# A recurrent attention with a gated feed-forward layer: the first running maxima spread from stacked halves, queries of one chunk instead of two in padded windows, and a new order

## The chip, the core and the metric

The kernel runs on one core of a Trainium2 chip. The core's engines work side by side, each through its own queue in strict program order: TensorE (PE in the profile; its weight loads are PEld) does matrix products and transposes into accumulators (PSUM), VectorE (DVE) and ScalarE (ACT) do elementwise work on accumulators and SBUF, GpSimd (POOL) does elementwise work on SBUF alone, SyncE (SP) issues most transfers. They wait for one another by semaphores. The metric is the device time of one execution in microseconds, the median of the runs.

## The reference

Inputs are q, k, v and an output gate, each [4 batches, 8 heads, 768 steps, 40], input and forget gates [4, 8, 768], and three feed-forward matrices. What matters of it:

```python
for t in range(S):
    m_new  = np.maximum(f_gate[:, :, t] + m, i_gate[:, :, t])
    f_stab = np.exp(f_gate[:, :, t] + m - m_new)
    i_stab = np.exp(i_gate[:, :, t] - m_new)
    C = f_stab * C + i_stab * outer(v[t], k[t])      # 40 x 40 for each batch and head
    n = f_stab * n + i_stab * k[t]
    y[t] = sigmoid(o_gate[t]) * (C @ q[t]) / max(|n . q[t]|, 1)
    m = m_new
x   = y as [4 * 768 tokens, 320]
out = (sigmoid(x @ w_gate) * (x @ w_val)) @ w_out    # 320 -> 1536 -> 320
```

## The kernel before

The 768 steps are cut into six chunks of 128. A unit is one batch in one chunk, numbered n = 4 * chunk + batch, so units 0 to 3 are chunk 0 and 4 to 7 chunk 1. In a unit the recurrence becomes products: scores of keys and queries (tile s), multiplied by a decay matrix d = exp(at - running maximum) with a triangular mask, and that times the values (tile av); from chunk 1 on the incoming state (tile cst) times the queries is added (tile in, the incoming term, line 740 on). The result is divided and gated (den, av, x), transposed (xt) and split into a high and a low part (xh, xl) of a type that TensorE takes in one pass. The feed-forward layer follows in tiles of 256 or 512 tokens: 16 or so products into two accumulators (pg, line 902), tanh on ScalarE and the gate product on VectorE (sg, lines 915 and 918), again a high and a low part (gh, gl), and the products with w_out (po, line 940). The weights arrive as 64-bit numbers and are decoded by ScalarE and VectorE (dc, lines 507 to 520) and split (wh, wl, w, oh, ol, lines 545 to 567).

The heads of 40 columns stand in three groups of 3, 3 and 2, so that a group fills 120 or 80 of the 128 rows. For units below EU = 8 keys and queries are transposed on TensorE (line 605 for keys, 607 for queries). The queries of these units lie in a tile qpad with zeros around each head; a window of that tile, transposed, holds one head of a group and zeros for the others (function window), so that a group needs one transpose for keys and as many for queries as it has heads. Tile sop (names kq) holds both, and one score product does a whole group (lines 719 and 1049). The incoming term of these units takes one product per head (line 749). Later units get keys and queries turned by VectorE and by transfers through memory, and qk holds a whole group's queries at once; there the incoming term takes one product per group (line 746), because cst has zeros between the heads.

At the start the gates of chunk 0 are summed up and their running maximum m0 (32 rows: batch and head) is found by scans on VectorE (gates_first). The maximum of a head is then spread to all 128 rows by a product with a column of the identity, four heads to an accumulator (function spread in opening, line 1024, tiles mb), from which ScalarE makes the decay (line 1029). TensorE gets products on a zero tile between its first real ones (keep_warm, `iq`, line 1003, twelve pairs of records; warming, `im`, six products).

Nothing is scheduled while it runs. Every step is put in a list under a key (`put`), and the table ORDER names the keys in the order in which the instructions are issued. PARAM['eng'] says for a step which engine does it: `v` VectorE, `a` ScalarE, `p` GpSimd.

Of the kernel before, what the change touches and what calls it, by code (L numbers as in the profile page):

```python
# [1151 lines left out]
```

## Time and profile before

| | us |
|---|---|
| median of 3 runs | 522.73 (522.59 to 523.77) |
| the profiled execution | 523.94 |
| its span, first to last instruction | 522.2 |
| TensorE busy | 514.5 |
| VectorE busy | 315.2 |
| ScalarE busy | 208.3 |
| GpSimd busy | 159.9 |

The profiled execution took 1.74 us more than its span and 1.2 us more than the median. In the views a row of the timeline gives a start, a duration, the engine, the line of the kernel, the operation, output and inputs with shapes, and a count of records. TensorE's records of one product overlap, so that the spacing in the chain of waits, not the duration of a record, is what a product costs in a row of them. An ordinary 32-bit product leaves two records, a transpose one.

### The profile page before, as it was taken

To read this page: it belongs to the slowest core of one execution; us is meant where nothing else is said; L and a number is where in the kernel's file an instruction comes from. 1 tells how busy PE (TensorE), PEld (TensorE's weight loads), DVE (VectorE), ACT (ScalarE), POOL (GpSimd) and SP (SyncE) were. 2 spreads that over 40 slices of the span, in tenths; PEclk is the share of its full clock that TensorE was granted. 3 is DMA by queue.
4 is the path that set the end of the run, shared out by engine and by line. 5 is a ranking of instruction groups with operands and counts; after the bars stand their busy time and mean duration, and the time that the engine had idled before them with its cause. 6 is when DMAs were issued, how large, how long until landed. Compare 5 with 4: busy or idle time off the path is not lost.

```text
span 522.2 us, 12322 instructions
## 1 busy us (share of the span) xinstructions
PE 514.5 (99%) x4747; PEld 468.6 (90%) x4747; DVE 315.2 (60%) x746; ACT 208.3 (40%) x535; POOL 159.9 (31%) x220
## 2 busy tenths in 40 slices
PE   8999999999999999999999999999999999999997
PEld 7788988888999999998888888898888888999997
DVE  6999879886556657656647544555456444342222
ACT  4786576673441433342433341223423131222321
POOL 3433244146444122305234425233322121202110
PEclk9999999999999999999999999999999999999999
DMA  8977776586778598688958799686689741000000
GB/s 197 239 223 195 196 199 211 134 156 130 183 147 188 125 196 165 162 155 177 187 139 184 156 178 198 150 179 126 142 173 191 162 87 48 28 13 2 32 9 25
DMA packets 227578, 75.55 MB, mean 145 GB/s; under 512 B 207040, under 2 KB 215424, under 8 KB 227520
## 3 DMA queue, kind: packets, MB, share of 16 engines
q1 hardware_dynamic: 226432, 74.51, 64.1%
q8 instruction: 37, 0.61, 0.5%
q10 hardware_dynamic: 1088, 0.26, 0.3%
q14 instruction: 21, 0.17, 0.1%
HBM read 57.61 MB, written 17.14 MB: 143 GB/s over the span
## 4 chain that ended last, share of the span: by engine, by line
PE 94%; DVE 3%; DMA 1%; issue 1%; POOL 0%; ACT 0%; DVEq 0%; POOLq 0%
PE pg L902 52%; PE po L940 25%; PE av L702 3%; PE s L724 2%; PE cs L855 2%; PE in L746 2%; PE s L719 1%; PE xt L820 1%; PE in L749 1%; PE pt L607 1%; PE mb L1024 1%; DMA d<-mscr 1%; PE s L1049 1%; DMA gin<-in_f_gate_dram 1%; PE pt L605 0%
## 5 line engine op out<-in xcount | busy, mean ns | idle before, releaser
L915 ACT ACTIVATE sg<-pg 128x256 f32<-128x256 f32 (+1 forms) x103 | 48.4, 470 | 211.6 <-PE pg L902 196.4
L929 POOL TENSOR_TENSOR gl<-sg,gh 128x256 fp32r<-128x256 f32 (+1 forms) x54 | 54.3, 1005 | 199.5 <-ACT gh L923 94.5
L918 DVE SCALAR_TENSOR_TENSOR sg<-sg,pg 128x256 f32<-128x256 f32 (+1 forms) x103 | 53.9, 523 | 95.8 <-ACT sg L915 54.1
L902 PE MATMUL pg<-xh,wh 128*128 128x256 f32 (+1 forms) x412 | 109.5, 336 | 0.1
L902 PE MATMUL pg<-xh,wl 128*128 128x256 f32 (+1 forms) x412 | 107.7, 328 | 0.0
L902 PE MATMUL pg<-xl,wh 128*128 128x256 f32 (+1 forms) x412 | 105.7, 329 | 0.0
L940 PE MATMUL po<-oh,gh 128*128 128x320 f32 x288 | 88.5, 321 | 0.0
L940 PE MATMUL po<-oh,gl 128*128 128x320 f32 x288 | 86.8, 317 | 0.0
L940 PE MATMUL po<-ol,gh 128*128 128x320 f32 x288 | 86.1, 314 | 0.0
L902 PEld LDWEIGHTS pg<-xh,wl 128*128 128x128 f32 x412 | 70.0, 188 | 5.2
L902 PEld LDWEIGHTS pg<-xl,wh 128*128 128x128 f32 x412 | 68.9, 188 | 5.2
L902 PEld LDWEIGHTS pg<-xh,wh 128*128 128x128 f32 x412 | 69.1, 188 | 4.8 <-DVE sg L918 0.3
L902 PE MATMUL pg<-xl,w 128*128 128x256 f32 (+1 forms) x206 | 62.0, 331 | 0.0
L940 PEld LDWEIGHTS po<-oh,gh 128*128 128x128 f32 x288 | 53.2, 188 | 3.8
L940 PEld LDWEIGHTS po<-ol,gh 128*128 128x128 f32 x288 | 53.2, 188 | 3.5
L940 PEld LDWEIGHTS po<-oh,gl 128*128 128x128 f32 x288 | 53.1, 188 | 2.9
L902 PE MATMUL pg<-xh,w 128*128 128x256 f32 (+1 forms) x206 | 54.4, 330 | 0.0
L923 ACT ACTIVATE gh<-sg 128x256 fp32r<-128x256 f32 (+1 forms) x65 | 32.2, 495 | 45.0 <-DVE sg L918 28.1
L730 DVE TENSOR_TENSOR d<-s,d 128x384 f32<-128x384 f32 (+1 forms) x66 | 32.8, 506 | 26.3 <-PE s L724 22.9
L462 ACT ACTIVATE d<-d,at 128x128 f32<-128x128 f32 x136 | 42.4, 391 | 0.1
L929 DVE TENSOR_TENSOR gl<-sg,gh 128x256 fp32r<-128x256 f32 (+1 forms) x49 | 28.6, 584 | 17.8 <-ACT gh L923 9.3
L902 PEld LDWEIGHTS pg<-xl,w 128*128 128x128 f32 x206 | 36.9, 188 | 1.8
(162 smaller groups left out, 728.1 us busy)
## 6 DMA issues: line engine op xcount, KB each, us to landing
d<-mscr SPq DMA_DIRECT2D x22, 512.0 KB
k<-in_k_dram SPq DMA_DIRECT2D x24, 160.0 KB
v<-in_v_dram SPq DMA_DIRECT2D x24, 160.0 KB
o<-in_o_gate_dram SPq DMA_DIRECT2D x24, 160.0 KB
st_o<-in_moe_w_out_dram SPq DMA_DIRECT2D x12, 320.0 KB
scr0q<-qt SPq DMA_DIRECT2D x32, 120.0 KB
...
```

The costliest lines, as they stand in the source:

```text
L462: nc.scalar.activation(d[:, h, :], d[:, h, :], AF.Exp, bias=at[:, c, b * H + h : b * H + h + 1], scale=-1.0)
L702: nc.tensor.matmul(dst[xs], lhs[:, xs], rhs, start=True, stop=True)
L724: nc.tensor.matmul(ps[g][:, m, :], ks[: 3 * D, h0 + m, :], qs[: 3 * D, h0 + m, :], start=True, stop=True)
L730: nc.vector.tensor_tensor(x, ps[g][:, :nh, :], x, ALU.mult)
L746: nc.tensor.matmul(pi[:, h0 : h0 + nh, :], qk[u][:r, g, :], cst[:r, b, g, : nh * DA], start=True, stop=True)
L855: nc.tensor.matmul(ps[0][:r, g, : nh * DA], kt[u][:, h0 : h0 + nh, :].rearrange("p h d -> p (h d)"), vt[u][:, h0 : h0 + nh, :], start=True ...
L902: nc.tensor.matmul(pg[x], w[:, a, fs] if a < 2 else w[:, fs], y[c][:, a, n0:n1], start=first, stop=a == 2 and y is xl)
L915: nc.scalar.activation(sg[0], pg[0], AF.Tanh, scale=0.5)
L918: nc.vector.scalar_tensor_tensor(sg[0], sg[0], 1.0, pg[1], ALU.add, ALU.mult)
L923: nc.scalar.activation(gh[u][:, :nt], sg[0], AF.Copy)
L929: E('gl0' if c == 0 else 'gl', f'tl{n}').tensor_tensor(gl[u][:, :nt], sg[0], gh[u][:, :nt].bitcast(F32), ALU.subtract)
L940: nc.tensor.matmul(po[t], g[c, j, t0][:, (t - t0) * P : (t - t0 + 1) * P], o[:, j, :], start=j == 0 and first, stop=j == NF - 1 and last)
```

## The change

1. *First maxima.* The running maximum is stored twice in a tile mm of the single-pass type: rows 0 to 31 hold its rounded value, rows 32 to 63 the rest (steps `ih`). A selector pick2 has a one in row h and in row 32 + h (step `iy`), so that one product with it adds both parts and spreads a head's maximum.
2. *Queries.* PU = 4 is new: only units 0 to 3 use padded windows. For units 4 to 7 a group's queries are transposed once, copied to qk, and multiplied by the mask rmask (one value per row and head of the group) into sop (steps `aq`); scores work as before. Their incoming term takes one product per group, and line 749 goes.
3. *Masks.* The mask cmask for the state is replaced by rmask, broadcast.
4. *Warm products.* keep is 7 instead of 12, warm 1 instead of 6.
5. *Order.* ORDER is a new table, with nine more steps than before (fifteen new, six gone), and 267 entries of PARAM['eng'] differ.

```diff
     'eng': {
...
-        'cm1': 'a', 'cp00': 'a', 'cp02': 'a', 'qb2': 'v', 'ro': 'v', 'xd0': 'v', 'bk0': 'v', 'cx0': 'p', 'bk1': 'v',
+        'cm1': 'a', 'cp00': 'v', 'cp02': 'v', 'qb2': 'v', 'ro': 'v', 'xd0': 'v', 'bk0': 'v', 'cx0': 'p', 'bk1': 'v',
...
-            if x < PARAM['EU']:
+            if x < PARAM['PU']:
                 return qpad[x % 2]
-            s = x % 6
+            s = (x - PARAM['PU']) % 6
...
+    mm = const.tile([P, L], F32R, name="mm")
+    pick2 = const.tile([P, BH], F32R, name="pick2")
...
+        def halves():
+            nc.vector.tensor_copy(mm[:BH], m0[:BH])
+
+        def rest():
+            nc.vector.tensor_tensor(mm[BH : 2 * BH], m0[:BH], mm[:BH].bitcast(F32), ALU.subtract)
...
-        for m in range(nh):
-            nc.tensor.transpose(p[:r, 1 + m, :], window(u, g, m), ident)
+        nc.tensor.transpose(p[:r, 0, :], heads(kt), ident)
+        if padded(u):
+            for m in range(nh):
+                nc.tensor.transpose(p[:r, 1 + m, :], window(u, g, m), ident)
+        else:
+            nc.tensor.transpose(p[:r, 1, :], heads(qt), ident)
...
+            pairs = [(sop[u][:r, g, 0], p[:r, 0]), (qk[u][:r, g], p[:r, 1])]
+        for dst, part_ in pairs:
+            if eng == "v":
+                nc.vector.tensor_copy(dst, part_)
+            else:
+                nc.scalar.activation(dst, part_, AF.Copy)
+
+    def spread(u, g, key):
+        nh = GROUPS[g][1]
+        r = nh * D
+        E(f'qb{g}', key).tensor_tensor(sop[u][:r, g, 1 : 1 + nh, :], qk[u][:r, g, :].unsqueeze(1).broadcast_to([r, nh, L]),
+                                      rmask[:r, :nh].unsqueeze(2).broadcast_to([r, nh, L]), ALU.mult)
...
-                if u in qk:
-                    nc.tensor.matmul(pi[:, h0 : h0 + nh, :], qk[u][:r, g, :], cst[:r, b, g, : nh * DA], start=True, stop=True)
-                    continue
-                for m in range(nh):
-                    nc.tensor.matmul(pi[:, h0 + m, :], sop[u][:r, g, 1 + m, :], cst[:r, b, g, m * DA : (m + 1) * DA],
-                                     start=True, stop=True)
+                nc.tensor.matmul(pi[:, h0 : h0 + nh, :], qk[u][:r, g, :], cst[:r, b, g, : nh * DA], start=True, stop=True)
...
-                cm = cmask.rearrange("p j e -> p (j e)")[:r, :w].unsqueeze(1).broadcast_to([r, ng, w])
-                nc.vector.tensor_tensor(tmp, ps[0][:r, gs, :w], cm, ALU.mult)
+                nj = w // DA
+                cm = rmask[:r, :nj].unsqueeze(1).unsqueeze(3).broadcast_to([r, ng, nj, DA])
+                nc.vector.tensor_tensor(tmp.rearrange("p g (j e) -> p g j e", e=DA),
+                                        ps[0][:r, gs, :w].rearrange("p g (j e) -> p g j e", e=DA), cm, ALU.mult)
...
+        def pairs():
+            nc.vector.memset(mm.bitcast(F32), 0.0)
+            nc.vector.memset(pick2.bitcast(F32), 0.0)
+            for x in range(2):
+                xs = slice(x * BH, (x + 1) * BH)
+                nc.vector.tensor_copy(pick2[xs], ident[xs, xs])
...
-                nc.tensor.matmul(p[:, j, :], ident[:, bh : bh + 1].broadcast_to([P, P]), m0, start=True, stop=True)
+                nc.tensor.matmul(p[:, j, :], pick2[:, bh : bh + 1].broadcast_to([P, P]), mm, start=True, stop=True)
```

How the program's order moves on two engines. VectorE at the start, before (gin holds the gates, m_99 the first maxima, at the transposed gates; a scan shows as SCALAR_TENSOR_TENSOR):

```order
L1122 SCALAR_TENSOR_TENSOR gin<-ones,gin 32x128
L1122 TENSOR_TENSOR gin<-gin 32x128
L1122 SCALAR_TENSOR_TENSOR m_99<-gin,mend 32x128
L1122 SCALAR_TENSOR_TENSOR gin<-mg,gin 32x128
L1122 TENSOR_TENSOR gin<-gin 32x128
L421 COPY at<-pt_ia__152 128x32
```

The same place in the changed program (mm the stacked halves, pick_100 the selector):

```order
L1163 SCALAR_TENSOR_TENSOR gin<-ones,gin 32x128
L1163 TENSOR_TENSOR gin<-gin 32x128
L353 MEMSET qpad_89 128x8x80
L1023 MEMSET mm 128x128
L1024 MEMSET pick_100 128x32
L1027 CAST pick_100<-ident 32x32 x2
L1163 SCALAR_TENSOR_TENSOR gin<-mg,gin 32x128
L1163 SCALAR_TENSOR_TENSOR m_98<-gin,mend 32x128
L406 CAST mm<-m_98 32x128
L435 COPY at<-pt_ia__148 128x32
L1163 TENSOR_TENSOR gin<-gin 32x128
L409 TENSOR_TENSOR mm<-m_98,mm 32x128
```

The scan of the first maxima stands behind five more instructions and a scan of the next gates, and the halves follow it. ScalarE at the start, before (dc are weights being decoded, d the decay, mb the spread maxima):

```order
L1122 DMA gin<-in_i_gate_dram 32x768
L344 DMA qpad_89<-in_q_dram 128x8x40
L1029 ACT_TABLE_LOAD
L1029 ACTIVATE d_0_112<-mb_0_159,at 128x128 x4
L507 ACTIVATE dc_0_185<-st_0_135 128x512
L507 ACTIVATE dc_0_201<-st_0_131 128x512
L1029 ACTIVATE d_0_112<-mb_1_173,at 128x128 x4
```

And in the changed program:

```order
L1163 DMA gin<-in_i_gate_dram 32x768
L348 DMA qpad_89<-in_q_dram 128x8x40
L521 ACT_TABLE_LOAD
L521 ACTIVATE dc_0_190<-st_0_132 128x512
L1070 ACTIVATE d_0_113<-mb_1_185,at 128x128 x4
L1070 ACTIVATE d_0_113<-mb_0_196,at 128x128 x4
L647 ACTIVATE kq_0_223<-pt_0_0_218 120x512
```

A decoding step now stands ahead of the first exponentials. TensorE at the incoming term of unit 4, before:

```order
L902 MATMUL pg_0_2_2_974<-xl_454,wh_102 128x256 x2
L902 MATMUL pg_0_2_2_992<-xh_450,wh_105 128x256
L749 MATMUL in_0_994<-cst,kq_0_885 128x41 x8
L902 MATMUL pg_0_2_2_992<-xh_450,wh_105 128x256
L902 MATMUL pg_0_2_2_992<-xh_450,wl_106 128x256 x2
```

And in the changed program:

```order
L937 MATMUL pg_0_1_2_914<-xl_447,w_105 128x256
L431 MATMUL pt_k__949<-ident,gin 128x32
L783 MATMUL in_0_953<-cst,qc_0_876 128x123 x2
L783 MATMUL in_0_953<-cst,qc_0_876 128x82
L937 MATMUL pg_0_1_2_921<-xl_447,w_108 128x256
```

Eight products of 41 columns became three of 123, 123 and 82, and they stand one feed-forward tile earlier.

## Rows read from the trace of the kernel before

**Rows 1.** The page: busy us of the engines; granted TensorE clock in 40 slices.
```profile
PE 514.5 (99%) x4747; PEld 468.6 (90%) x4747; DVE 315.2 (60%) x746; ACT 208.3 (40%) x535; POOL 159.9 (31%) x220
...
PEclk9999999999999999999999999999999999999999
```

**Rows 2.** The page: the chain that ended last, by engine.
```profile
PE 94%; DVE 3%; DMA 1%; issue 1%; POOL 0%; ACT 0%; DVEq 0%; POOLq 0%
```

**Rows 3.** The chain in order of time, opening: start, us, what.
```profile
5.46 1.71 PE mb L1024 x8
...
13.30 0.89 PE mb L1024 x8
...
21.96 1.06 DVE dc L516
...
42.06 0.50 DVE x L795
...
42.70 0.67 PE s L719 x2
```

**Rows 4.** Windows: stretch, length, busy us by engine, clock, DMA share, GB/s.
```profile
10.00:52.25 42.25, 40.00 (x508) 33.98 (x507) 40.17 (x107) 32.63 (x90) 16.01 (x26) 1.00 0.84 216
52.25:100.00 47.75, 47.75 (x365) 41.63 (x367) 40.77 (x101) 31.23 (x76) 15.93 (x20) 1.00 0.69 189
...
100.00:150.00 50.00, 49.98 (x512) 45.80 (x506) 33.96 (x83) 25.09 (x65) 24.46 (x28) 1.00 0.74 156
```

**Rows 5.** The chain in order of time, units 4 to 9.
```profile
50.09 1.44 PE pg L902 x12
51.53 0.11 PE pt L605
51.64 0.22 PE pt L607 x2
...
56.69 1.71 PE in L749 x16
...
145.32 0.63 PE in L746 x6
```

**Rows 6.** Groups of one form on VectorE: count, busy us, mean ns.
```profile
L730 DVE TENSOR_TENSOR d<-s,d 128x384 f32<-128x384 f32 x44 | 23.9, 549 | 17.8 <-PE s L724 15.2 <-PE s L719 2.3
```

**Rows 7.** Timeline of VectorE: start, us, line, operation, shapes.
```profile
4.08 0.28 DVE L1122 TENSOR_TENSOR gin<-gin 32x128 f32<-32x128 f32 x1
4.46 0.47 DVE L1122 TENSOR_TENSOR_SCAN m<-gin,mend 32x128 f32<-32x128 f32 x1
...
5.49 0.17 DVE L421 COPY at<-pt_ia__152 128x32 f32<-128x32 f32 x1
...
9.14 0.59 DVE L349 MEMSET qpad<- 128x640 f32 x1
...
25.25 1.16 DVE L547 CAST w<-dc 64x256 fp32r<-64x256 f32 x2
...
51.23 0.85 DVE L565 TENSOR_TENSOR w<-dc,w 64x256 fp32r<-64x256 f32 x2
...
52.25 0.41 DVE L918 SCALAR_TENSOR_TENSOR sg<-sg,pg 128x256 f32<-128x256 f32 x1
...
99.89 0.68 DVE L918 SCALAR_TENSOR_TENSOR sg<-sg,pg 128x512 f32<-128x512 f32 x1
```

**Rows 8.** Timeline: a shift beside GpSimd's low part, and one alone.
```profile
21.57 1.27 POOL L561 TENSOR_TENSOR wl<-dc,wh 128x512 fp32r<-128x512 f32 x1
21.87 1.15 DVE L516 TENSOR_SCALAR dc<-dc 128x320 int32<-128x320 int32 x1
...
39.63 0.31 DVE L516 TENSOR_SCALAR dc<-dc 128x320 int32<-128x320 int32 x1
```

**Rows 9.** Timeline of ScalarE: first exponentials and first decodings.
```profile
7.21 1.14 ACT L1029 ACTIVATE d<-mb,at 128x128 f32<-128x128 f32 x4 [0.18 <-PE mb L1024]
8.59 1.24 ACT L507 ACTIVATE dc<-st 128x512 f32<-128x512 f32 x2 [0.24 <-DMA st<-in_moe_w_val_dram]
```

More of the change, by code (lines that the diff above doesn't have):

```diff
@@ L28 @@
         'qb00': 'v', 'qb01': 'v', 'qb02': 'v', 'qb10': 'v', 'qb11': 'v', 'qb12': 'v', 'cm0': 'a', 'arg1': 'a',
[4 rows of a table removed]
[4 rows of a table added]
         'cr2': 'p', 'cx2': 'p', 'zm2.1': 'v', 'aq3.0': 'v', 'ah3.1': 'a', 'aq3.1': 'v', 'cr3': 'p', 'zm3.1': 'v',
[66 rows of a table removed]
[72 rows of a table added]
     },
-    'warm': 6,
+    'warm': 1,
     'AV': 4,
@@ L105 @@
     'TS': False,
-    'keep': 12,
+    'keep': 7,
     'EU': 8,
+    'PU': 4,
 }
 ORDER = """
-w26f w25f w29f w28f w21f iw it if ii lq0 iq lk0 ib iq x0 iq x1 v1 lk1 ir lq1 ig v0 ig lv0 ig ia iq gc lo0 sp00 gc
-iac g ex00 iq sp01 mk00 ig gc*3 ip g wva ip x2 tr00 tr01 wga wgb*2 wvb iq x4 ex01 cp01 tr02 tr11 g lo1 igs cp02
-sp10 / sc01 cp00 cp11 lk2 is mk01 ex10 lq2 bk0 ti01 wvb wgb sp11 sc00 ex11 lv1 sc02 ti00 tr10 wgd mk11 ti02 c0 tr12
-wvb mk10 ic ld2 cp10 cv0*2 wge sc11 ct0 ct1 x3 wgf cp12 sc10 bk1 wra a2.2 cv0 ti11 wrb a2.0 w3a ah2.2 sc12 ah2.0 z1
@@ L249 @@
[L249 to L253 removed]
+w26f w25f w29f w28f w21f iw it if ii lq0 iq lk0 ib iq x0 iq x1 v1 lk1 lq1 ig v0 ig lv0 ia iq ip ir is iy gc ig ih
@@ new lines @@
+t12 p11 t12 w25b p11 dy4 t12 al8.0 z5 zm5.1 w25b ta12 w26a p11*2 as8.0 t12 w25d w26b w24e e7 p11 c5 ld8 as8.1 w25e
+p11 p10*2 t13 as8.3 p11 lk9 zd4.0 cs5 cv5 tg12 cg5 cv5*2 cr5 cx5 t13*5 za4.0 w27a th12 p11 t13*2 zm5.0 w26b w27b
+p11 t13*3 / a6.1 p12 t13*3 tl12 w29a w27b w26b t13 p12 ta13 w29b w27b w29b w24f za5.1 ah6.1 w26d w27d d5 p12*2
+as8.2 p12 t13 t14 lv6 p12 w26e tg13 th13 dx5 e8 ct7 p12 ci6 t14*3 p11 p12 lo8 lq10 tl13 p12 t14*2 w27e zd6.0 w28a
+t14*4 p12 cf6 aq6.1 t14 dy5 t14 lv9 aq8 t14 w28b zd6.1 w29b lq9 t14 p13*2 t14 aq8 lq12 aq8 t14 / a7.2 p13 ta14
@@ new lines @@
+t25 as11.3 as10.6 th24 t25 p23 t25*2 tl24 t25*7 / ci9 t25 ta25 p24 cv8 tg25 zd9.1 cf9 p24 bk9 v11 zd9.0 p24 p23
+t26*2 p23*2 as10.4 t26 th25 t26*3 lq13 cr8 tl25 t26 / b9.0 t26 bm9.0 ah12.0 t26*2 al12.0 as11.2 t26*2 p25 t26*2
+as11.0 aq10 p24 t26 ta26 p25 p24*2 b9.2 t26 tg26 t27 as11.1 t27 bm9.2 th26 t27*3 b9.1 cx8 tl26 bm9.1 t27 s10 t27*2
+s10 p25*2 t27*2 s10 p26 t27*4 p25 t27*2 p26 d8 ta27 tg27 dx8 c9 p26 aq11*2 t28*2 dy8 th27 aq10 s10 t28 p25 p26
+t28*3 e11a tl27 t28*3 cs9 cv9 a11.1 p26 t28*5 cg9 t28 p26 ta28 z9 t28 tg28 p27 zm9.0 th28 ah11.1 za8.1 tl28 za9.0
@@ new lines @@
+al12.1 t34 tg33 th33 e11 e11m t34*2 e12m / c10 dx9 dy9 cs10 ld13 p32 t34*6 lq14 as12.0 t34*2 tl33 cv10 lv11 t34*3
+cv10 t34 p32 ta34 t34 p33*3 cv10 a13.0 tg34 p33 t35 cg10 bk11 t35 p33 ah13.0 th34 p33 t35*8 tl34 p34 t35*5 p34
+as12.6 t35 p34 ta35 ci11 lo11 tg35 t36 th35 cf11 t36*9 al13.0 tl35 t36 p34 t36*4 p35 t36 p34*2 / b11.0 ta36 tg36
+t37*4 th36 oh5 t37*4 lo12 o5 t37*3 bm11.0 tl36 p35 t37*3 p35 t37*2 p35 p36*3 ta37 p35*2 tg37 as13.3 t38 p36 lv15
+lo13 th37 t38*3 tl37 cr10 cx10 t38*5 as12.7 as12.5 t38*2 p36 as12.4 aq12 t38 / b11.2 p36 bm11.2 aq12 t38*4 p37*2
@@ new lines @@
+cs14 t52*4 cv14 t52 v16 cv14 zd14.1 cv14 za14.1 cg14 t52 al17.0 t52 cr14 t52*2 ta52 p50 ci15 p50 tg52 p50*2 zd15.1
+p50 bk16 p50*2 t53 cx14 zd15.0 as16.0 as16.1 th52 t53 p51 zd14.0 cf15 ld17 lo17 a18.0 p51 t53 d14 t53*5 ah18.0
+za14.0 p50 tl52 t53*3 p51 p52 dx14 aq16 p52 dy14 al18.0 aq16 p51*5 p52 aq16 p52 p51 t53*5 b15.2 bm15.2 p51 ct15
+ta53 b15.0 p51 tg53 p51 b15.1 th53 bm15.1 s16 t54*2 bm15.0 p52 t54 a17.1 t54*2 / c15 ah17.1 t54 al17.1 cs15 t54*2
+tl53 t54*3 p53 t54*3 cv15*2 cg15 cv15 cr15 cx15 t54 ta54 z15 p53 ct17 lk18 d15 p52 zm15.1 p52 ld18 p53 s16*2 p53
@@ new lines @@
+bk19 p61 ta63 p61 e20a e20 p61 b18.1 al20.0 bm18.1 p61 p62*2 p61*2 p62*2 as20.3 t64 / b18.0 aq19 t63 bm18.0 aq19
+t64 s19 t64 p62*2 s19*2 as20.2 cf18 tg63 t64 th63 tl63 t64 / c18 cs18 p62 t64 s19 t64 cg18 a21.0 ld22 as20.1 t64
+as20.7 as20.4 cv18 p63 cv18 d17 t64 p62 cv18 dx17 dy17 cr18 p63 t64*5 p63 t64*2 p63 / z18 p63 cx18 ah21.0 as20.6
+as20.5 ta64 p63 p62*2 zm18.0 ci19 zm18.1 tg64 p62 p63 th64 p63*3 d18 zd18.1 za18.0 t65 za18.1 dx18 al21.0 cf19
+t65*2 tl64 t65*2 lo20 t65*2 dy18 lk21 t65*4 as20.0 t65*4 p64*4 b19.0 t65 b19.1 p63 ta65 bm19.0 t66 tg65 b19.2 t66
@@ new lines @@
+t95*2 th94 t95*3 tl94 t95*10 p93 p94*2 t95 p93 ta95 p93*2 tg95 t96*2 p94 t96*7 p94 t96 th95 tl95 t96*6 p95 ta96
+p95*2 p94 tg96 p94 t97*2 th96 t97*4 tl96 t97*3 p95 t97*2 p96 t97*5 ta97 p95*2 p96*2 tg97 p96 t98*2 th97 p96 t98*3
+tl97 t98*10 p97 t98 ta98 p97*2 p96 p97 tg98 t99*2 th98 t99*5 tl98 t99*8 p98 ta99 p97 t99 p98 p97 tg99 th99 t100*7
+tl99 t100*8 p98*2 p99 ta100 t100 p98*2 tg100 th100 t101*16 tl100 ta101 p99*3 tg101 p99 p100 t102*2 th101 t102 p99
+t102*3 tl101 t102*9 p100*2 t102 p100*2 p101 p100 p101*5 ta102 tg102 th102 tl102 p102*5 oh22 p102 oh23 o22 o23
@@ L368, in mlstm_then_gated_ffn_kernel @@
     ones = const.tile([BH, L], F32, name="ones")
-    cmask = const.tile([P, 3, DA], F32, name="cmask")
     rmask = const.tile([P, 3], F32, name="rmask")
@@ L398, in gates_first @@
         gate_max("ig", 0)
+        def halves():
+            nc.vector.tensor_copy(mm[:BH], m0[:BH])
+        def rest():
+            nc.vector.tensor_tensor(mm[BH : 2 * BH], m0[:BH], mm[:BH].bitcast(F32), ALU.subtract)
+        put("ih", halves)
+        put("ih", rest)
     def gates_of(key, c0, c1):
@@ L600, in mlstm_then_gated_ffn_kernel, with padded @@
     qk, sop, xin = {}, {}, {}
+    def padded(u):
+        return u[0] * B + u[1] < PARAM['PU']
     def turned(u, g, p):
@@ L604, in turned, with heads @@
         r = nh * D
-        nc.tensor.transpose(p[:r, 0, :], kt[u][:, h0 : h0 + nh, :].rearrange("p h d -> p (h d)"), ident)
-        for m in range(nh):
-            nc.tensor.transpose(p[:r, 1 + m, :], window(u, g, m), ident)
+        def heads(t):
+            return t[u][:, h0 : h0 + nh, :].rearrange("p h d -> p (h d)")
+        nc.tensor.transpose(p[:r, 0, :], heads(kt), ident)
[4 more added lines that the diff above has]
+            nc.tensor.transpose(p[:r, 1, :], heads(qt), ident)
     def copied(u, g, p, eng):
@@ L613, in copied @@
         r = nh * D
-        if eng == "v":
-            nc.vector.tensor_copy(sop[u][:r, g, : 1 + nh], p[:r, : 1 + nh])
-        else:
-            nc.scalar.activation(sop[u][:r, g, : 1 + nh], p[:r, : 1 + nh], AF.Copy)
+        if padded(u):
+            pairs = [(sop[u][:r, g, : 1 + nh], p[:r, : 1 + nh])]
+        else:
+            if u not in qk:
+                qk[u] = two.tile([P, 3, L], F32, tag="qk", name="qc_%d_%d" % u)
+            pairs = [(sop[u][:r, g, 0], p[:r, 0]), (qk[u][:r, g], p[:r, 1])]
[9 more added lines that the diff above has]
+                                      rmask[:r, :nh].unsqueeze(2).broadcast_to([r, nh, L]), ALU.mult)
     xh, xl = {}, {}
@@ L668, in st_a @@
                 put(f"ah{n}.{g}", copy, g)
+                if not padded(u):
+                    put(f"aq{n}.{g}", spread, u, g, f"aq{n}.{g}")
         else:
@@ L977, in resets @@
             nc.gpsimd.memset(mend[:, 0:1], -1e30)
-            nc.gpsimd.memset(m0, 0.0)
             nc.gpsimd.memset(rst, 1.0)
@@ L986, in small_masks @@
                                     fill=0.0, base=-(L - 1), channel_multiplier=1)
+        def pairs():
[4 more added lines that the diff above has]
+                nc.vector.tensor_copy(pick2[xs], ident[xs, xs])
+        put("iy", pairs)
         put("ir", resets)
@@ L990, in opening @@
         put("ib", nc.gpsimd.memset, ones, 1.0)
-        put("ic", block_mask, cmask, DA)
         put("is", small_masks)
```

250 lines of the change are left out of this document (110 added, 140 removed), and 142 rows, old and new, of the table PARAM.

## The prediction

> **What bounds the kernel now.** I read the page's busy shares first, then the chain of waits by engine, then the same chain in order of time, and last the timelines of the engines that the chain leaves. TensorE is busy 514.5 of 522.2 us, no other engine more than 60% [rows 1]. The chain that ended last lies 94% on TensorE [rows 2]. One product less there is therefore time saved, wherever TensorE is the one that others wait for. The chain in order of time says where that is not so: from 21.96 to 42.06 us its pieces are mostly VectorE's, and from 42.70 us on they are TensorE's [rows 3]. VectorE is busy 40.17 of the 42.25 us up to 52.25 us, still 40.77 of 47.75 us after it, and 33.96 of 50 us after 100 us [rows 4]. So there are two regions: an opening that VectorE bounds, and from about 50 us a long stretch that TensorE bounds, the first half of it with little slack on VectorE.
>
> **The change, part by part.** The first two parts are certain.
>
> *Three heads at once, units 4 to 7.* The incoming term of such a unit is eight products of 41 columns and takes 1.71 us of TensorE; the same term of a later unit, already done with three products, takes 0.63 us [rows 5]. All four lie behind 50 us, where TensorE is the bound: 4 × (1.71 − 0.63) = 4.32 us less.
>
> *Fewer transposes in the same units.* A transpose costs 0.11 us (0.22 for two) [rows 5]. A unit needs three for keys and now three instead of eight for queries, five less, 0.55 us. Unit 4's fall before 52 us, where VectorE bounds; those of units 5 to 7 count: 15 × 0.11 = 1.65 us. Together 5.97 us that nothing hides.
>
> *The queries are spread by a mask instead.* Twelve products with a mask come in, nine on VectorE and three on GpSimd by the program's order. No row shows one; the nearest is the 128x384 product with scores, 549 ns on VectorE [rows 6]. From above 0.6 us, from below 0.3: I take 0.5, 4.5 us on VectorE between 50 and 115 us, off TensorE's path as long as VectorE keeps up. The copies out of the accumulators become two per group where there was one; most are ScalarE's, which is busy 31.23 of 47.75 us there [rows 4].
>
> *First maxima, one product each.* On TensorE the four groups now take 1.71 us early and 0.89 us later [rows 3]. A single pass of 256 columns of the other type costs 0.12 us (1.44 for 12) [rows 5]; with 128 columns four of them cost between 0.24 and 0.48 us. That frees about 3.5 us of TensorE, and with the keep-warm pairs, the warm products and unit 4 some 6 us in all, but in the opening, where TensorE waits anyway: I count it at nothing. Its cover is VectorE; were that gone, it would count.
>
> *VectorE in the opening.* By the program's order 124 instructions stand up to the gate product of the fifth tile (at 52.25 us [rows 7]) before, and 127 now. Away go three pairs of weights' low parts (0.85 a pair) and a pair of casts (1.16) [rows 7], and a scaling of keys worth about 0.45 (between half a pair and the 128x384 product [rows 6]): 4.2 us. In come six small ones for the halves and the selector (between 0.17, a copy of 32 columns, and 0.28, a 32x128 subtraction [rows 7], so 1.0 to 1.7; most are smaller still, I take 1.0), one decode step, one low part, two casts and two copies of 128 columns (0.28 to 0.55 each, I take 0.33: 2.0). Net −1.2 us, between −1.5 and +0.8.
>
> *GpSimd in the opening.* What VectorE loses GpSimd gets: some five more operations with two inputs before 52 us. While GpSimd made a low part from 21.57 us, VectorE's shift of 128x320 took 1.15 us; alone it takes 0.31 [rows 8]. One more such meeting costs 0.84 us, five would cost 4.2, none 0; GpSimd was at such work nine times in this stretch and few of VectorE's rows are stretched like that, so I take one: +0.8.
>
> The Trainium skill, "GPSIMD Engine Reference", section "8. Key points", says that GpSimd shares its SBUF interfaces with VectorE and contends with certain of its instructions; the rows agree. Read as "each meeting is paid in full" it would make the five cost 4.2 us, and the sum 3.4 us longer.
>
> *The first exponentials wait for more.* VectorE now runs a fill of the query tile (0.59), four small fills and casts (some 0.5) and a scan (0.4) ahead of the scan of the first maxima, which stood at 4.46 us [rows 7], and four short steps (0.9) behind it; the first spread product moves from 5.46 us [rows 3] to about 7.3. ScalarE has a new first instruction, the decoding of the first weights, ahead of the exponentials. Its data are there no later than 9.2 us, when the second of the two decodings began that started at 8.59 [rows 9]. Queued behind it on ScalarE are all 16 exponentials, then GpSimd's masks, and VectorE's scaling of keys, which stands in its queue in front of the score products. At worst the first exponentials go from 7.21 [rows 9] to 9.25 us, 2.0 us late; at best, with the shorter spread, nothing is lost. VectorE has other work ahead of that point, so I take +0.4.
>
> *The sum.* Opening: −1.2 + 0.8 + 0.4 = 0. The rest: −5.97. *New order* beyond that: the tail ends in the same kinds of instructions as before, and after 100 us VectorE is idle for a third of the time [rows 4], so that moving work between engines there costs nothing I can find. The profiled execution took 523.94 us with a span of 522.2; it becomes 518.0 with a span of 516.2. The median of the runs is 522.73, 1.2 us under the profiled one, and becomes 516.8 us.
>
> **The rivals.**
>
> *B, the opening gets longer.* The late first maxima and the weights in front of the exponentials are not absorbed: +2.0 us, 518.8. For it: VectorE runs strictly in its order, and its scaling of keys waits for exponentials and masks. Against: the chain shows no wait for ScalarE or GpSimd in the first 20 us, and the spread itself gets shorter by up to 1.2 us a group.
>
> *C, VectorE stays the bound until 100 us.* Between the gate products at 52.25 and 99.89 us [rows 7] TensorE loses two incoming terms and about ten transposes (2.2 + 1.1), so 44.5 us are left; VectorE's 40.8 us grow by about 2 (six of the masks 3.0, four more low parts of 128x512 against four pairs and casts less), to 42.8. That is 96%. If VectorE idles there as it does now, 7.0 us [rows 4], the stretch takes 49.8 us, 5.3 more than TensorE needs: 522.0. If half as long, 46.3: 518.5. Between: 519.5.
>
> *D, the opening gets shorter.* No new meetings with GpSimd and nothing late: −1.2 to −1.5 us, some 515.3. If TensorE's own work was the hidden bound in part of the opening, up to 3 us more, 512.3; I price it at 514.5.
>
> *E, slower.* TensorE falls to half rate in the opening. The same four products, eight records, take 1.71 us at 5.46 and 0.89 us at 13.30 [rows 3], that is 1.2 and 2.4 GHz, although the granted clock reads 1.0 in every slice [rows 1]; what lay between is a TensorE kept busy with keep-warm pairs. Now it has five pairs less, shorter spreads and more waiting. From 22 to 42.7 us, where VectorE leads the chain, TensorE's products take some 16.7 us by their spacing (an estimate: their number by 0.11 to 0.12 us, 0.65 for a score product). At half rate throughout these would take 33.4 us in a stretch of 20.7: +12.7, 529.5. It decides from 10 us of such products on: 4 us are slack and 6 us the gain. Against it: before, the pairs at 22 to 26 us were few, and the rate held through that stretch.
>
> The Trainium skill, "TensorE: Matmul & The Clock Gate", section "Part 1: The HAM clock gate (the "warmup" mystery)", states that the throttled state is the default and activity releases it. The trace agrees for the start; that TensorE falls back after waits of the length seen here, no run shows.
>
> That the change doesn't do what it says (the new product as dear as the old) costs nothing in the sum, since the opening is counted at nothing for TensorE.
>
> **How the numbers follow.** Forecast 516.8 with a chance of 0.50 (own range 514.8 to 518.2), B 0.15, C 0.18, D 0.11, E 0.06. A measurement of this kernel can't tell less than 0.3%, 1.6 us, from no change, so "faster" ends at 521.2 and "slower" begins at 524.3. Faster: 0.50 + 0.14 + 0.13 + 0.11 = 0.88; same, the upper ends of B and C: 0.06; slower, E: 0.06. The range of 8 in 10 leaves out E, the top of C and the far end of D: 512.8 to 521.0.
>
> **What would show it.** Incoming terms of units 4 to 7 at about 0.63 us, six transposes of 0.11 us in each of these units, spread groups under 0.5 us. Right: the first piece of the chain that is TensorE's for good still near 42 us, and the gate product of the fifth tile at 52 ± 1.5 us. B: that product later by 2 us, with ScalarE's first exponential after 9 us. C: VectorE pieces in the chain between 55 and 100 us. E: transposes of 0.21 us between 20 and 45 us. The forecast is wrong if TensorE's idle time, or its spacing of the same products, grows after 110 us, which I hold for untouched.

## The result, and the profile after

| | before | changed | ratio, 95% interval |
|---|---|---|---|
| first comparison | 523.25 us (522.59 to 523.78) | 517.29 us (516.90 to 518.02) | 0.9888 [0.9869, 0.9908] |
| again, beside the experiments | 523.33 us (522.17 to 526.16) | 516.49 us (515.95 to 517.97) | 0.9871 [0.9854, 0.9889] |

The kernel is 6.0 to 6.8 us faster; forecast were 516.8 us and 5.9 us. The profiled execution took 516.91 us with a span of 515.2, against 523.94 and 522.2. The page after, for [rows 1, 2]: busy time of the engines, the granted clock in 40 slices, the chain by engine.

```profile
PE 506.3 (98%) x4651; PEld 458.6 (89%) x4651; DVE 318.9 (62%) x772; ACT 201.9 (39%) x530; POOL 155.9 (30%) x216
...
PEclk9989999999999999999999999999999999999999
...
PE 94%; DVE 3%; ACT 1%; issue 1%; DMA 1%; POOL 0%; DVEq 0%; ACTq 0%
```

TensorE is busy 8.2 us less and VectorE 3.7 us more. One slice of the clock, the third, is new. The windows after, for [rows 4] (stretch, length, busy us by engine, clock, DMA share, GB/s):

```profile
10.00:52.25 42.25, 39.63 (x485) 33.22 (x484) 39.51 (x110) 34.43 (x97) 21.11 (x26) 0.96 0.89 223
52.25:100.00 47.75, 47.75 (x397) 41.04 (x396) 45.08 (x107) 33.57 (x92) 18.47 (x24) 1.00 0.74 198
100.00:150.00 50.00, 50.00 (x521) 46.33 (x519) 37.96 (x89) 24.37 (x67) 27.58 (x34) 1.00 0.85 168
```

From 52.25 to 100 us VectorE went from 40.77 to 45.08 of 47.75 us, and still TensorE has no gap: it never waits there, but VectorE has only 2.7 us left. The chain in order of time after, for [rows 3, 5] (start, us, what):

```profile
7.51 1.97 PE mb L1065 x8
...
28.20 0.64 PE pt L628 x3
...
30.20 0.33 PE pt L628 x3
...
42.02 0.23 DVE dc L526
...
44.10 0.82 PE av L740 x64
...
53.89 0.83 PE in L783 x6
...
88.02 0.63 PE in L783 x6
```

The incoming terms of units 4 and 5 take 0.83 and 0.63 us where a unit took 1.71. The same three transposes take 0.64 us at 28.20 and 0.33 us at 30.20: between about 25 and 29 us TensorE ran at half rate. VectorE hands the chain to TensorE for good at 44.10 us. VectorE's own rows, for [rows 6, 7]: the mask products by form (count, busy us, mean ns), and the fifth tile's gate product in the timeline.

```profile
L652 DVE TENSOR_TENSOR kq<-qc,rmask 120x384 f32<-120x384 f32 x6 | 3.5, 584 | 0.3 <-ACT qc L647 0.3
...
L652 DVE TENSOR_TENSOR kq<-qc,rmask 80x256 f32<-80x256 f32 x3 | 1.2, 411 | 0.0
```
```profile
51.58 0.41 DVE L953 SCALAR_TENSOR_TENSOR sg<-sg,pg 128x256 f32<-128x256 f32 x1
```

### The profile page after: what moved, and what is told of

It is laid out like the page before. It is cut to its first block, busy times and chain, and to the rows that moved or that the text cites. A ratio compares the mean times of both kernels' runs of the same rounds, so it can differ in the third digit from the quotient of the medians.

```text
span 515.2 us, 12164 instructions
## 1 busy us (share of the span) xinstructions
PE 506.3 (98%) x4651; PEld 458.6 (89%) x4651; DVE 318.9 (62%) x772; ACT 201.9 (39%) x530; POOL 155.9 (30%) x216
## 4 chain that ended last, share of the span: by engine, by line
PE 94%; DVE 3%; ACT 1%; issue 1%; DMA 1%; POOL 0%; DVEq 0%; ACTq 0%
PE pg L937 53%; PE po L975 25%; PE av L740 3%; PE in L783 3%; PE s L762 2%; PE cs L888 2%; PE s L757 2%; PE xt L853 1%; PE pt L628 1%; PE pt L625 1%; DMA gin<-in_f_gate_dram 1%; PE mb L1065 1%; POOL d L1075 0%; DVE dc L534 0%; DVE av L824 0%
## 5 line engine op out<-in xcount | busy, mean ns | idle before, releaser
L937 PE MATMUL pg<-xh,wl 128*128 128x256 f32 (+1 forms) x412 | 110.1, 331 | 0.0
L937 PE MATMUL pg<-xl,wh 128*128 128x256 f32 (+1 forms) x412 | 108.8, 332 | 0.0
L964 POOL TENSOR_TENSOR gl<-sg,gh 128x256 fp32r<-128x256 f32 (+1 forms) x43 | 42.9, 997 | 167.1 <-ACT gh L958 74.7
L975 PE MATMUL po<-ol,gh 128*128 128x320 f32 x288 | 88.7, 316 | 0.0
L975 PE MATMUL po<-oh,gl 128*128 128x320 f32 x288 | 88.2, 316 | 0.0
L937 PEld LDWEIGHTS pg<-xl,wh 128*128 128x128 f32 x412 | 70.4, 190 | 5.0
L937 PE MATMUL pg<-xl,w 128*128 128x256 f32 (+1 forms) x206 | 63.7, 336 | 0.0
L964 DVE TENSOR_TENSOR gl<-sg,gh 128x256 fp32r<-128x256 f32 (+1 forms) x60 | 34.1, 568 | 13.5 <-ACT gh L958 7.9
L958 ACT ACTIVATE gh<-sg 128x256 fp32r<-128x256 f32 (+1 forms) x58 | 28.2, 487 | 32.1 <-DVE sg L953 23.5
```

Source lines behind the costliest of these rows:

```text
L937: nc.tensor.matmul(pg[x], w[:, a, fs] if a < 2 else w[:, fs], y[c][:, a, n0:n1], start=first, stop=a == 2 and y is xl)
L958: nc.scalar.activation(gh[u][:, :nt], sg[0], AF.Copy)
L964: E('gl0' if c == 0 else 'gl', f'tl{n}').tensor_tensor(gl[u][:, :nt], sg[0], gh[u][:, :nt].bitcast(F32), ALU.subtract)
L975: nc.tensor.matmul(po[t], g[c, j, t0][:, (t - t0) * P : (t - t0 + 1) * P], o[:, j, :], start=j == 0 and first, stop=j == NF - 1 and last)
```

## The experiments

Each was timed beside the kernel before. Ratios are to that kernel; the changed kernel's is 0.9871, and "slower" or "faster than the changed kernel" means than its 516.49 us. Whole times hide effects of a microsecond, because the opening differs from run to run, for the most part with TensorE's clock (under *More pairs, fewer pairs*). So a second measure is taken from the timelines: the time from the first record of unit 4's incoming term to that of unit 8's. It lies behind the opening and is sharp, since kernels that do the same work there agree to 0.07 us (one profiled execution of each):

| kernel | unit 4 at | unit 8 at | between | against the changed kernel |
|---|---|---|---|---|
| changed, two runs | 53.82; 54.13 | 137.69; 138.00 | 83.87; 83.87 | 0 |
| more pairs; fewer pairs | 53.97; 54.06 | 137.77; 137.90 | 83.80; 83.84 | -0.07; -0.03 |
| maxima in two passes; decoding later | 52.81; 54.24 | 136.62; 138.06 | 83.81; 83.82 | -0.06; -0.05 |
| term by head | 54.09 | 142.42 | 88.33 | +4.46 |
| turned by head | 54.05 | 140.06 | 86.01 | +2.14 |
| masked twice | 52.93 | 140.68 | 87.75 | +3.88 |
| masks on GpSimd | 54.01 | 138.97 | 84.96 | +1.09 |
| before | 56.53 | 145.16 | 88.63 | other order |
| queries alone; with masks on GpSimd | 57.57; 57.83 | 143.31; 144.53 | 85.74; 86.70 | order of before |

**Once more, the changed kernel.** 

> The changed kernel once more, to narrow the interval of its ratio to the kernel before and to stand beside the experiments on the same chip. Expected 517.3 us, 0.9888 of before, within 0.3 %.

Measured 516.49 us, as expected within 0.3%.

**Term by head.**

```diff
+                if n < PARAM['EU']:
+                    for m in range(nh):
+                        nc.tensor.matmul(pi[:, h0 + m, :], qk[u][:r, g, :], cst[:r, b, g, m * DA : (m + 1) * DA],
+                                         start=True, stop=True)
+                    continue
                 nc.tensor.matmul(pi[:, h0 : h0 + nh, :], qk[u][:r, g, :], cst[:r, b, g, : nh * DA], start=True, stop=True)
```

> The changed kernel, with the incoming term of units 4 to 7 in eight products by head (16 records) in place of three (6 records); all else as it was. Theory (TensorE sets the pace after 52 us): 4 x (1.71 - 0.63) = 4.3 us slower than the changed kernel, 521.6 us. Rival (VectorE or the eviction of the term sets the pace for the units before 100 us, so that only the later two terms count): about 2.2 us slower, 519.5 us. If this part was worth nothing: 517.3 us.

Measured 521.59 us, ratio 0.9964 [0.9949, 0.9979], 5.1 us slower than the changed kernel. The chain of this kernel at unit 5, as above:

```profile
89.41 1.71 PE in L785 x16
```

The time between the two terms grows by 4.46 us for four units. Every one counts in full, also those before 100 us (1.10 to 1.13 us from each unit's term to the next). The theory holds.

**Turned by head.**

```diff
-            nc.tensor.transpose(p[:r, 1, :], heads(qt), ident)
+            for m in range(nh):
+                nc.tensor.transpose(p[:r, 1 + m, :], heads(qt), ident)
```

> The changed kernel, with the queries of units 4 to 7 transposed once for each head (3, 3 and 2 transposes for the three groups) in place of once for each group: 20 more transposes at 0.11 us. The further results are written to their bank and read by nobody. Theory: 15 of them stand where TensorE sets the pace, 1.65 us slower than the changed kernel, 519.0 us; all 20 counted, 2.2 us and 519.5 us. Rival (VectorE sets the pace up to 100 us): under 1.1 us slower, below 518.4 us.

Measured 519.33 us, ratio 0.9922 [0.9908, 0.9935], 2.8 us slower. Units 5 to 7, whose 15 extra transposes lie between the two terms, cost 2.14 us where 1.65 was expected. Up to unit 6's term it is 1.13 us for ten, as priced; the five of unit 7 cost 1.01. Of the further 0.5 us most is VectorE's: unit 7's mask product met GpSimd's work and took 2.13 us, where the same one took 0.70 us in the changed kernel,

```profile
121.07 2.13 DVE L653 TENSOR_TENSOR kq<-qc,rmask 120x384 f32<-120x384 f32 x1 [0.59 <-ACT qc L648]
```

and TensorE's next scores, at 124.33 us, came some 0.4 us later than the transposes alone put them, behind the row of VectorE's work that follows this product. So the price of a transpose was right. The theory holds.

**Masked twice.**

```diff
-                    put(f"aq{n}.{g}", spread, u, g, f"aq{n}.{g}")
+                    put(f"aq{n}.{g}", lambda g=g: [spread(u, g, f"aq{n}.{g}") for _ in range(2)])
```

> The changed kernel, with each of the 12 mask products done twice (the second writes the same values again): 9 more on VectorE at 0.55 us, 3 more on GpSimd at 0.82 us. Theory (VectorE has slack for them beside TensorE): within 0.5 us of the changed kernel, 517.3 to 517.8 us. Rival (VectorE, over 94 % busy from 52 to 100 us, sets the pace there): the 5 or 6 of them before 100 us count in full, 2.7 to 3.3 us slower, 520.0 to 520.6 us.

Measured 519.90 us, ratio 0.9930 [0.9918, 0.9943], 3.4 us slower; 3.88 us between the two terms. The theory fails, and the rival has the reason: VectorE had no room for them. What TensorE waited for from 50 to 150 us (line, releaser: us in total, times, longest), where the changed kernel has no such wait:

```profile
PE s L757 <- DVE d L768: 0.8, 2, 0.6
PE pt L625 <- DVE at L435: 0.5, 1, 0.5
PE pg L937 <- DVE sg L953: 0.3, 1, 0.3
```

All three releasers are VectorE's. The rival's sum came near in part by luck: it counted only the products before 100 us, and of the 3.88 us 2.1 lie between the terms of units 4 and 6 (up to 104.59 us) and 1.8 behind. The nine added products also cost VectorE more than the 0.55 us each that was expected: 18 took 12.8 us where nine took 4.7, the slowest of them beside GpSimd's work, which had three more as well. So this run shows that a second set finds no room; it does not price the first.

**Queries alone, in the order of before.** The first maxima, pairs, engines and the order of all other steps stay; each mask step stands right behind its eviction, as here for one group. By the engine table of before, eight of the products are VectorE's and four GpSimd's:

```diff
-w11b a4.0 w12d w12f tl3 ld5 lq5 w11b ah4.0 t4*8 g
+w11b a4.0 w12d w12f tl3 ld5 lq5 w11b ah4.0 aq4.0 t4*8 g
```

> The kernel before, in its own order, with the queries' part alone: units 4 to 7 are not padded, three heads at once, 12 mask products, each put right behind the eviction that it needs, and the incoming term in three products. First maxima, keep-warm pairs, engines and the order of all else stay as before. Theory (the gain is TensorE's work that is no longer there, and the order is worth little): 4.32 + 1.65 = 6.0 us faster than before, ratio 0.9886. Rival (without the new order the 12 mask products and the narrower evictions stand in VectorE's way up to 100 us): 2 to 4 us faster, ratio 0.992 to 0.996.

Measured 522.15 us, ratio 0.9980 [0.9968, 0.9992]: 1.2 us faster than before, below even the rival's range. The same TensorE work is gone as in the changed kernel, and 4.9 to 5.7 us of the gain with it. The windows of this kernel (columns as above):

```profile
52.25:100.00 47.75, 46.32 (x379) 39.60 (x379) 44.00 (x107) 30.73 (x80) 17.24 (x20) 0.96 0.67 176
100.00:150.00 50.00, 48.48 (x436) 43.98 (x437) 35.51 (x87) 24.64 (x70) 25.15 (x30) 1.00 0.80 162
```

TensorE idles for 1.43 and 1.52 us. Its longest waits from 50 to 150 us:

```profile
PE pg L922 <- DVE sg L938: 1.8, 1, 1.8
PE xt L840 <- DVE x L823: 1.2, 1, 1.2
PE s L744 <- DVE d L755: 1.0, 1, 1.0
```

The first ends at 52.69 us, mostly before the windows shown. TensorE waits there for a gate product behind this pair of weights' low parts, which took 0.85 us in the kernel before [rows 7] and meets a low part and a mask product of GpSimd's here:

```profile
49.96 2.10 DVE L566 TENSOR_TENSOR w<-dc,w 64x256 fp32r<-64x256 f32 x2
```

After it the granted clock was 0.50 from about 53 to 56 us (the 0.96 of the first window), another 1.7 us or so of TensorE's work (an estimate: half of 3.4 us). For the wait of 1.0 us, the chain in order of time where it leaves TensorE:

```profile
76.62 0.12 PE pt L617
...
77.29 0.80 DVE kq L639
...
78.29 0.47 DVE kq L639
...
79.56 0.47 DVE kq L639
...
85.45 0.56 DVE d L755
86.06 0.91 PE s L744 x2
```

Transposes release VectorE at 76.74 us, VectorE works off three mask products and the decodings that stand behind them without a gap, and its product with the scores at 85.45 us, the last of that row, releases TensorE's next scores. The kernel before has the same row; in the timeline there it begins and ends so, and TensorE's scores follow:

```profile
77.28 0.55 DVE L615 COPY kq<-pt 80x384 f32<-80x384 f32 x1 [0.53 <-PE pt L607]
...
78.75 0.28 DVE L516 TENSOR_SCALAR dc<-dc 128x256 int32<-128x256 int32 x1
...
84.72 0.55 DVE L730 TENSOR_TENSOR d<-s,d 128x384 f32<-128x384 f32 x1
...
85.61 0.81 PE L719 MATMUL s<-kq 120*128 120x384 f32 x2
```

From 77.28 to 84.72 us VectorE had one wait, of 0.17 us, and TensorE's scores began 0.34 us after its last product ended (84.72 + 0.55), without a wait. Inside this row a shorter TensorE could gain 0.34 us and no more; at its head VectorE waits 0.53 us for TensorE's transposes, so that the row could begin that much sooner. Beyond these 0.87 us the row of VectorE is the path, and the mask products make it longer: 8.0 us from 77.28 to the end of the product with the scores before, 9.2 us from 76.77 here.

**Queries alone, masks on GpSimd.** As the last, with the masks' engine changed:

```diff
+        'aq4.0': 'p', 'aq4.1': 'p', 'aq4.2': 'p', 'aq5.0': 'p', ... 'aq7.2': 'p',
```

> The kernel before with the queries' part alone in its own order, as in the earlier run of that name, but all 12 mask products on GpSimd. There VectorE led the chain from 76.8 to 85.5 us with the mask products (0.47 to 0.80 us each) and the decodings queued behind them, and TensorE stood idle about 3 us between 52 and 150 us. Theory (the mask products' time on VectorE is what eats the gain in that order): most of it comes back, 4 to 6 us faster than before, ratio 0.9885 to 0.992. Rival (the place of evictions and products in the old order, on whichever engine): 1 to 2.5 us faster, ratio 0.995 to 0.998.

Measured 522.34 us, ratio 0.9987 [0.9977, 0.9997], no better: 0.8 us faster than before, just below the rival's range. By the trace the run did not separate the two, because the masks came back to VectorE in another way. Its timelines of GpSimd and VectorE:

```profile
78.74 0.74 POOL L731 TENSOR_TENSOR k<-k,d 128x320 f32<-128x320 f32 x1
79.44 1.61 POOL L640 TENSOR_TENSOR kq<-qc,rmask 120x384 f32<-120x384 f32 x2
...
78.82 2.37 DVE L518 TENSOR_SCALAR dc<-dc 128x256 int32<-128x256 int32 x1
```

The shift that took 0.28 us in the kernel before takes 2.37 us beside a scaling of keys and two mask products on GpSimd; 2.1 us lost, more than the three mask products cost VectorE in the run before (0.80 + 0.47 + 0.47). Whether another place for the masks in the old order would have kept the gain was not tried.

**Masks on GpSimd, in the new order.** The same edit in the changed kernel.

> The changed kernel with all 12 mask products on GpSimd (9 of them at 0.55 us leave VectorE, where doubling them had cost about 3 us). Theory (in the new order VectorE is just in time: TensorE has no idle stretch from 52 to 150 us, so freeing VectorE gives nothing more): within 0.5 us of the changed kernel, 516.5 to 517.3 us. Rival (VectorE still sets the pace there): 2 to 3 us faster, about 514.5 us. The other side: GpSimd takes 0.82 us for one and the scores wait for it, 1 to 2 us slower.

Measured 518.29 us, ratio 0.9915 [0.9902, 0.9928], 1.8 us slower, 1.09 us of it between the two terms: the other side, though not by the way that was named. GpSimd's and VectorE's timelines:

```profile
113.94 1.28 POOL L965 TENSOR_TENSOR gl<-sg,gh 128x512 fp32r<-128x512 f32 x1
115.18 1.08 POOL L498 TENSOR_SCALAR_AFFINE_SELECT d<-d 128x1024 f32<-128x1024 f32 x1
116.24 0.86 POOL L582 TENSOR_TENSOR ol<-dc,oh 128x320 fp32r<-128x320 f32 x1
...
114.61 2.76 DVE L909 TENSOR_TENSOR cst<-cst,ct 120x246 f32<-120x246 f32 x1
```

An addition of 445 ns (mean of the same form in the changed kernel; this one took 0.65 us there) takes 2.76 us, with GpSimd at work beside it from 113.94 to 117.10 us. TensorE waits twice for VectorE's gate product, 1.8 us together. The other wait, 0.92 us, ends at 52.28 us, ahead of unit 4's term: a decoding step of VectorE's that took 0.68 us in the changed kernel took 1.88 from 49.78 us, beside two mask products on GpSimd (1.46 us from 49.65).

**Engines of before, in the new order.** Only the table of engines is exchanged.

```diff
-        'cm1': 'a', 'cp00': 'v', 'cp02': 'v', 'qb2': 'v', 'ro': 'v', 'xd0': 'v', 'bk0': 'v', 'cx0': 'p', 'bk1': 'v',
+        'cm1': 'a', 'cp00': 'a', 'cp02': 'a', 'qb2': 'v', 'ro': 'v', 'xd0': 'v', 'bk0': 'v', 'cx0': 'p', 'bk1': 'v',
...
```

> The changed kernel in its new order, with the table of engines of the kernel before (which of VectorE, ScalarE and GpSimd takes the decoded weights, the copies and the subtractions). Theory (the order of the steps is what makes room for the mask products): within 1 us of the changed kernel, 516.5 to 517.5 us. Rival (the new choice of engines does): 2 to 5 us slower, 519 to 522 us.

Measured 534.44 us, ratio 1.0220 [1.0205, 1.0235]: some 18 us slower than the changed kernel and 11 slower than before, far outside both expectations. The chain by engine:

```profile
PE 78%; DVE 10%; issue 4%; ACT 4%; POOL 2%; DMA 1%; POOLq 0%; DVEq 0%; ACTq 0%
```

TensorE's share fell from 94% to 78%. The order and the table of engines go together: each engine works its queue in order, and TensorE now waits for ScalarE, GpSimd and VectorE in turn, in many places. So this run can't say which of the two made the room; it says that the order does not without its table. The table in the old order was not run.

**More pairs, fewer pairs.** In the order, behind the first unit's last transposes:

```diff
-d0 iq*2 wre
+d0 iq*6 wre
```

> The changed kernel, with four more keep-warm pairs behind the two that stand after the first unit's last transposes (at 22 us), where TensorE otherwise sits idle from 22.95 to 24.1 us and its granted clock falls to half from about 25.5 to 28.9 us. Theory (VectorE sets the pace up to 44 us, and so the half clock costs nothing): within 0.5 us of the changed kernel. Rival (the products done at half clock between 25.5 and 28.9 us, 3.4 us of work that would take 1.7, delay everything behind them): the clock stays whole and the kernel is 1.0 to 1.7 us faster, about 515.9 us.

> The changed kernel without the two keep-warm pairs that stand behind the first unit's last transposes at 22 us; TensorE is then idle there for 0.9 us more. Theory (VectorE sets the pace up to 44 us, and a half clock for some microseconds before that costs nothing): within 0.5 us of the changed kernel, even if the half clock lasts longer. Rival (the half clock reaches further and its products delay the rest): each microsecond of products at half clock costs one more, 1 to 4 us slower, 517.7 to 521 us.

 (There the edit takes `iq*2` out.)

Measured 516.67 us, 0.9867 [0.9852, 0.9882], with more pairs; 517.62 us, 0.9897 [0.9883, 0.9911], with fewer. The windows of the changed kernel, then of the one with more pairs, then with fewer (columns as above; the clock is the third value from the end; the changed kernel's is 0.50 from 26 to 29 us):

```profile
22.00:25.00 3.00, 1.79 (x13) 1.24 (x12) 2.97 (x10) 2.88 (x10) 1.76 (x4) 1.00 1.16 303
```
```profile
22.00:25.00 3.00, 2.49 (x28) 1.60 (x28) 2.86 (x10) 2.95 (x11) 1.91 (x4) 1.00 1.11 279
...
27.00:28.00 1.00, 0.91 (x6) 0.70 (x7) 1.00 (x4) 1.00 (x4) 0.38 (x1) 1.00 0.54 113
```
```profile
22.00:25.00 3.00, 0.80 (x20) 0.48 (x11) 2.86 (x10) 2.95 (x10) 1.84 (x5) 1.00 1.14 258
...
27.00:28.00 1.00, 1.00 (x6) 0.94 (x6) 1.00 (x5) 1.00 (x5) 0.29 (x1) 0.50 0.63 97
```

With more pairs the clock stays whole, and nothing is won; with fewer it falls as in the changed kernel, and unit 4's term starts at 54.06 us, between the two runs of the changed kernel. Its higher median can't be told from their 516.49 and 517.29. Both times are as the theory has them, but they don't show that the half clock costs nothing. The chain of the run with more pairs goes through the added pairs:

```profile
22.53 0.54 PE xt L853 x3
...
25.54 0.49 PE pkeep10x L1044 x2
26.03 0.34 PE xt L853 x3
```

Four pairs take 2.2 us, where TensorE had waited 1.15. Its next transposes begin at 25.86 us; in the second run of the changed kernel, which stands level with this one up to there, they begin at 24.95. The pairs cost 0.9 us, and the whole clock gave it back.

What the half clock costs shows beside the run with masks twice: it has the changed kernel's program up to 50 us, and its clock stayed whole. A window and two rows of VectorE, of the changed kernel and then of that run:

```profile
25.00:30.00 5.00, 4.88 (x29) 4.45 (x28) 4.45 (x14) 3.89 (x10) 3.15 (x2) 0.66 0.96 244
...
25.46 0.54 DVE L866 TENSOR_TENSOR xl<-xt,xh 128x384 fp32r<-128x384 f32 x1
...
30.42 0.42 DVE L953 SCALAR_TENSOR_TENSOR sg<-sg,pg 128x256 f32<-128x256 f32 x1 [0.94 <-ACT sg L950]
```
```profile
25.00:30.00 5.00, 4.70 (x38) 4.15 (x38) 4.95 (x15) 4.75 (x12) 3.71 (x2) 1.00 0.90 228
...
25.63 0.54 DVE L866 TENSOR_TENSOR xl<-xt,xh 128x384 fp32r<-128x384 f32 x1
...
29.58 0.40 DVE L953 SCALAR_TENSOR_TENSOR sg<-sg,pg 128x256 f32<-128x256 f32 x1
```

At 25.5 us the changed kernel is 0.17 us ahead; at its gate product it is 0.84 us behind, because that product waits for TensorE's, and unit 4's term follows 0.89 us later (53.82 for 52.93). The runs with maxima in two passes and with masks on GpSimd, whole too, have that gate product at 29.44 and 29.51 us. From 26.06 to 37.02 us the chain of the changed kernel is TensorE's. So the half clock cost 0.9 to 1.0 us. Whole times say the same: the changed kernel's two executions with a mean granted clock of 1.00 took 515.95 and 516.25 us, its other six, at 0.995 to 0.997, 516.73 to 518.02. With the term by head five at 0.999 or 1.00 took 520.76 to 521.59 us, four at 0.996 or 0.997 522.18 to 522.51. The theory's reason fails; the rival had the cost right, and added pairs were no remedy.

**Maxima in two passes.**

```diff
-                nc.tensor.matmul(p[:, j, :], pick2[:, bh : bh + 1].broadcast_to([P, P]), mm, start=True, stop=True)
+                nc.tensor.matmul(p[:, j, :], ident[:, bh : bh + 1].broadcast_to([P, P]), m0, start=True, stop=True)
```

> The changed kernel, with the first maxima spread from the whole f32 rows again (32 records in place of 16, the zeroing of their tile on GpSimd again); the stacked halves are still made and not used. Theory (the opening is bound by VectorE, so this part was worth nothing): within 0.5 us of the changed kernel. Rival (the first exponentials wait for them and the masks, products and scores wait for those): the first two groups take 1.7 us more at half clock, and the kernel is 1.0 to 1.7 us slower, 518.3 to 519.0 us.

Measured 516.78 us, ratio 0.9877 [0.9858, 0.9897], no difference. In this run the exponentials begin at 9.10 us (8.67 in the changed kernel), and unit 4's term all the same at 52.81 us. That 1.0 to 1.3 us is no gain of the edit's: the run with masks twice, whose opening is the changed kernel's, shows 52.93; in both the clock stayed whole. The theory holds.

**Decoding later.**

```diff
-sp01 wga ex01
+sp01 ex01 wga
```

> The changed kernel, with the first weight decoding on ScalarE (0.67 us, at 7.75 us) moved behind the first group of exponentials, which stood ahead of it in the kernel before and started 1.46 us sooner there. Theory (VectorE sets the pace of the opening with work that does not wait for these exponentials): within 0.5 us of the changed kernel. Rival (the later exponentials cost the opening what they are late): 0.5 to 0.7 us faster, 516.6 to 516.8 us. The other side: VectorE's decodings now start 0.7 us or more later and the kernel is slower by up to 2 us.

Measured 516.56 us, ratio 0.9866 [0.9849, 0.9882], no difference. ScalarE's timeline of this kernel:

```profile
8.70 1.14 ACT L1070 ACTIVATE d<-mb,at 128x128 f32<-128x128 f32 x4 [0.35 <-PE mb L1065]
```

The exponentials begin at 8.70 us, no sooner than with the decoding ahead of them (8.67). They are late because they wait for the spread products, which start at 7.51 us in the changed kernel and 7.54 here. So the edit did not bring them forward, and the run doesn't test what their delay costs. The run with maxima in two passes, where they begin 0.4 us later still, lost nothing by it.

None of these kernels beats the changed one clear of the noise.

## Why the prediction was right, and where it was not

- *Incoming term, 4.32 us.* Right: undone, it costs 4.46 us behind the opening. That it lies on TensorE's path even before 100 us is what the run shows.
- *Transposes, 1.65 us.* Right in price. Undone they cost 2.14 us, of which some 0.4 us is a mask product of VectorE's that met GpSimd's work. Undone, the two parts together cost 6.6 us against the 5.97 that were called certain.
- *"Together 5.97 us that nothing hides."* This is where the working failed, though the total came out. In the order of before the same cut brings 1.2 us (522.15 for 523.33). The page and the windows [rows 1, 4] showed a busy TensorE, and from that I took each microsecond less as time saved. The timeline showed the row of VectorE from 77.28 to 84.72 us whose last product TensorE's scores follow by 0.34 us; it was there to read.
- *Mask products at nothing.* The durations were right (0.41 and 0.58 us for the 0.5 taken, nine on VectorE, three on GpSimd). Their price was not: doubled, they cost 3.88 us. That one set is free in the new order rests on TensorE's having no wait from 52 to 150 us; no run takes the set away.
- *"New order: costs nothing I can find", and nothing gained.* The step that failed most. Between the queries alone (522.15 us) and the changed kernel (516.5 to 517.3) lie 4.9 to 5.7 us, and two of the other differences, the first maxima and the pairs at 22 us, are worth nothing by their runs, in the new order; what is left is the order with its engines, and the warm products and the broadcast mask, which no run undoes. Two terms of opposite sign had been left out, and that they cancelled was luck: what stood in the way in the old order, where 1.2 of 5.97 us came through (+4.8: VectorE's rows with the mask products, and in the profiled execution a stretch at half clock behind one of the waits), and the new order with its engines (about -5, by subtraction; no run has it alone).
- *Rival C* (VectorE stays the bound to 100 us, 519.5) described the mechanism of the queries alone rightly, except that VectorE there has 44.00 us of work in 47.75 and TensorE waits for its order, not for its sum. In the changed kernel it did not happen: no VectorE piece leads the chain between 55 and 100 us.
- *The opening, net 0.* Right within its range, but made of two terms that were not in the sum: the gate product of the fifth tile came at 51.58 us for 52 ± 1.5, the first spread product at 7.51 for 7.3, the first exponentials at 8.67 between 7.21 and 9.25. The step behind the last was wrong: I had them wait for the decoding, and they wait for the spread. With the clock whole the same gate product came at 50.70 us (masks twice) and 50.57 (maxima in two passes), some 1.6 us before the 52.25 of before, as in rival D; the half clock took back about 1 us, as in rival E. VectorE hands over the chain for good at 44.10 us, not near 42.
- *First maxima at nothing.* Right, by the run that undoes them. The sign for them, groups under 0.5 us, did not show: the first two take 1.97 us together at 7.51 us, at half rate.
- *Rival E* (half rate) came true for some 3.4 us and cost 0.9 to 1.0 us. The 4 us of slack under which it was to cost nothing were not there: 3.4 us at half rate are 1.7 us more for the same products (an estimate), and VectorE's gate product at 30.42 us waited 0.94 us for them. That VectorE leads up to 42.7 us was read from the kernel before; in the changed one TensorE leads from 26.06 to 37.02. That TensorE falls back after such waits, which no run had shown, this one shows.
